# Turning pooled keys and values outside TensorE: block turns, small transfers and the DMA crossbar

## The chip, the cores and the metric

One core of a Trainium2 chip. The metric is the device time of one execution in microseconds (us), median of several runs; lower is better. "The profile" is one profiled execution, "the trace" is what its views are read from. PE is TensorE, PEld its weight loads, DVE VectorE, ACT ScalarE, POOL GpSimd, SP the queue that issues most transfers. A turn is a transposition. The crossbar is the way by which a transfer turns its data (`dma_start_transpose`). The record of an instruction is the duration that the trace gives it, and a transfer has landed when its completion semaphore is full.

## The reference, cut to what matters

```python
B, C, Hh, Ww = (4, 128, 384, 32)          # q: (4, 12288, 128), kv: (4, 384, 32, 128)
kv_pool = kv.reshape(B, H // 4, 4, W // 4, 4, C).mean(axis=(2, 4))
kv_flat = kv_pool.reshape(B, -1, C) @ w_sr               # 768 keys per batch
k = v = kv_flat
a = softmax(q @ k.T / sqrt(C));  x = a @ v               # 49152 tokens of 128
out = (relu(x @ w_gate) * (x @ w_val)) @ w_out           # d_ff = 1536
```

## The kernel before

Tokens go through in 96 tiles of 512, one per loop iteration of 12 steps. A step holds a value and a gate projection, an output product, and scores or attention values. The next batch's keys are prepared on the side, two chunks of 128 keys (a "pair") at a time, three pairs per batch. GpSimd sums the 16 pixels of a key. TensorE turns the sums (`turn_add`), projects them (`project`) and turns the projected keys into values (`turn_values`). Each result goes back from PSUM through VectorE.

```python
def kv_load(b, pair, ...):                  # four transfers of 512 KB, on SP
    ...
        nc.sync.dma_start(parts[:, dh].rearrange("p h dw c -> p (h dw c)"), rows[dh])

def turn_add(b, pair, lines, first, final, chunks=(0, 1)):      # float32, 2 turns for a pair
    ...
            nc.tensor.matmul(kv_Ts[b, pair][:, h], lines[:, h, i], ident, is_transpose=True, ...)
    ...
        nc.vector.tensor_copy(kvT, kv_Ts[b, pair])

def project(b, pair):
    pr = bank([128, 2, 128])
    nc.tensor.matmul(pr, w_sr_f32, kv_Ts.pop((b, pair)), start=True, stop=True)
    nc.vector.tensor_scalar(kv16[:, b, 2 * pair : 2 * pair + 2, 0:C], pr, 1.0 / (r * r), ...)

def turn_values(b, pair):
    vt = bank([128, 2, 128], FP16)
    for h in range(2):
        nc.tensor.transpose(vt[:, h], kv16[:, b, 2 * pair + h, 0:C], ident16)
    nc.vector.tensor_copy(kv16[:, b, 2 * pair : 2 * pair + 2, C : 2 * C], vt)

def x_turn(k):                              # attention output of a tile, by the crossbar, on SP
    ...
    nc.sync.dma_start_transpose(xT, x16.rearrange("p s c -> p (s c)"))

# in the loop (at counts iterations: 0 is where the next batch's keys begin)
if step == 1 and 0 <= at < NJC and at % 2 == 0:
    kv_load(b, at // 2)
if step == 3 and 0 <= at - 2 < NJC:
    pool_pixels(nc.gpsimd, b, (at - 2) // 2, at % 2)
pair = (at - 5) // 2
if at % 2 == 1 and 0 <= pair < NJC // 2:
    if step == 2: turn_open(b, pair); turn_add(b, pair, s3s.pop((b, pair))[:, :, None], True, True)
    if step == 4: project(b, pair)
    if step == 8: turn_values(b, pair)
```

The softmax here doesn't subtract the row's maximum and nothing guards it: scores larger than these inputs give would overflow.

## Time and profile before

| | before |
|---|---|
| time, median of 3 runs | 1048.1 us (1048.07 to 1048.92) |
| span of the profiled run | 1045.5 us, granted TensorE clock 1.000 |
| ordinary iteration | 10.51 us |
| iteration with a pair's turns and projection (nine of them) | 11.28 us |

How to read it: the prediction below shows the lines, and how they say that the time is the length of TensorE's instruction stream.

### The profile page before, as it was taken

Reading aid. Unit: us, or ns where it says so; the run is one execution under the profiler, and the core shown is the slowest. Engines: PE = TensorE matmul, PEld = TensorE weight load, DVE = VectorE, ACT = ScalarE, POOL = GpSimd, SP = SyncE. Lnnn points to the kernel's source line nnn. Section 1 sums busy time; section 2 is a strip of 40 time slices with the busy share of each in tenths; the row PEclk is TensorE's granted clock in tenths of the full one; section 3 lists DMA queues with packets and bytes.
Section 4 is the critical chain, followed back from the end, with each engine's and each line's share of the span. In section 5 each row is a group of like instructions: output and inputs, shape, how many; then the busy total and the mean of one; then the engine's idle time right before and its main releaser. Section 6 shows DMA issues by size and latency. Waiting matters only on the chain.

```text
span 1045.5 us, 25976 instructions
## 1 busy us (share of the span) xinstructions
PE 1036.0 (99%) x9984; PEld 690.1 (66%) x9984; DVE 913.3 (87%) x1679; ACT 908.9 (87%) x1741; POOL 107.8 (10%) x127
## 2 busy tenths in 40 slices
PE   8999999999999999999999999999999999999998
PEld 6566666666666666666666666666666666666665
DVE  3798889898988888998888888889988888888898
ACT  3888888888888888888888888888888888888887
POOL 2000045200000015500000003440000000000000
PEclk9999999999999999999999999999999999999999
DMA  8733256241422335623224134551331322212111
GB/s 302 120 82 74 79 177 167 52 87 32 87 53 65 72 125 138 157 57 72 58 60 87 31 87 132 150 150 41 77 65 53 72 65 54 67 32 67 32 47 47
DMA packets 125853, 90.75 MB, mean 87 GB/s; under 512 B 103328, under 2 KB 104224, under 8 KB 125728
## 3 DMA queue, kind: packets, MB, share of 16 engines
q1 hardware_dynamic: 120144, 75.78, 26.8%
q0 software_dynamic: 5440, 13.24, 7.7%
q8 instruction: 78, 1.28, 0.5%
q14 instruction: 47, 0.39, 0.1%
q10 hardware_dynamic: 144, 0.07, 0.0%
HBM read 52.76 MB, written 25.17 MB: 75 GB/s over the span
## 4 chain that ended last, share of the span: by engine, by line
PE 97%; DMA 1%; SPq 1%; DVE 0%; ACT 0%; issue 0%; DVEq 0%
PE bank_ps L257 25%; PE bank_ps L247 24%; PE bank_ps L236 24%; PE bank_ps L198 12%; PE bank_ps L187 12%; DMA parts<-in_kv_dram 1%; PE bank_ps L156 1%; PE bank_ps L168 1%; SPq L128 0%; ACT aT L188 0%; SPq L93 0%; PE bank_ps L176 0%; DVE kv L169 0%; DVE kvT L163 0%; PE bank_ps L229 0%
## 5 line engine op out<-in xcount | busy, mean ns | idle before, releaser
L250 DVE SCALAR_TENSOR_TENSOR hT<-bank_ps,val 128x512 f16<-128x512 f32 x1152 | 759.5, 687 | 100.9 <-ACT val L240 74.7
L240 ACT CAST val<-bank_ps 128x512 f16<-128x512 f32 x1152 | 677.7, 591 | 111.8 <-PE bank_ps L236 107.5
L257 PEld LDWEIGHTS <-hT 128*128 128x128 f16 x4608 | 351.4, 98 | 200.1 <-issue 0.9
L257 PE MATMUL bank_ps<-wo,hT 128*128 128x128 f16 x4608 | 443.1, 219 | 0.0
L236 PE MATMUL bank_ps<-xT,wv 128*128 128x512 f16 x1152 | 436.6, 379 | 0.0
L247 PE MATMUL bank_ps<-xT,wg 128*128 128x512 f16 x1152 | 435.7, 378 | 0.0
L188 ACT ACTIVATE aT<-bank_ps 128x512 f16<-128x512 f32 x576 | 346.0, 604 | 16.9 <-PE bank_ps L187 16.6
L198 PE MATMUL bank_ps<-kv,aT 128*128 128x129 f16 x2304 | 223.3, 219 | 0.0
L198 PEld LDWEIGHTS <-aT 128*128 128x128 f16 x2304 | 177.2, 98 | 68.1 <-issue 0.6
L187 PE MATMUL bank_ps<-qT,kv 128*128 128x512 f16 x576 | 216.4, 379 | 1.1 <-DVE kv L169 0.5
L247 PEld LDWEIGHTS <-wg 128*128 128x128 f16 x1152 | 111.5, 97 | 65.8 <-issue 0.5
L236 PEld LDWEIGHTS <-wv 128*128 128x128 f16 x1152 | 112.7, 98 | 0.5
L214 DVE TENSOR_TENSOR x<-bank_ps,rinv 128x256 f16<-128x256 f32 x188 | 79.7, 424 | 6.7 <-DVE rinv L206 0.2
L78 POOL DMA_DIRECT2D q<-in_q_dram x23 | 12.5, 545 | 570.6 <-DMA qT<-q 570.4
L275 DVE TENSOR_SCALAR o_sb<-bank_ps 128x512 f32<-128x512 f32 (+1 forms) x95 | 64.0, 674 | 1.3 <-PE bank_ps L257 1.3
L139 POOL TENSOR_TENSOR s<-parts 128x512 f32<-128x512 f32 x36 | 45.3, 1269 | 162.7 <-DMA parts<-in_kv_dram 153.5
L187 PEld LDWEIGHTS <-kv 128*128 128x128 f16 x576 | 55.8, 98 | 2.4 <-DVE kv L169 1.4
L206 DVE RECIPROCAL rinv<-bank_ps 128x2 f32<-128x2 f32 x192 | 30.6, 160 | 1.6 <-PE bank_ps L198 1.6
L141 POOL TENSOR_TENSOR s<-s 128x512 f32<-128x512 f32 x18 | 22.9, 1269 | 1.4
L143 POOL TENSOR_TENSOR c<-s 128x256 f32<-128x256 f32 x18 | 13.1, 726 | 1.4
L163 DVE COPY kvT<-bank_ps 128x256 f32<-128x256 f32 x12 | 5.0, 417 | 4.5 <-PE bank_ps L156 4.5
L146 POOL TENSOR_TENSOR kv_s<-c 128x128 f32<-128x128 f32 x18 | 8.2, 456 | 1.4
(37 smaller groups left out, 81.0 us busy)
## 6 DMA issues: line engine op xcount, KB each, us to landing
parts<-in_kv_dram SPq DMA_DIRECT2D x48, 512.0 KB, 6.4
out_dram<-o_sb SPq DMA_DIRECT2D x95, 256.0 KB, 2.1
q<-in_q_dram POOLq DMA_DIRECT2D x23, 512.0 KB, 5.1
xT<-x SPq DMA_TRANSPOSE x94, 2.5
q<-in_q_dram SPq DMA_DIRECT2D x1, 768.0 KB, 8.3
wv<-in_moe_w_val_dram POOLq DMA_DIRECT2D x2, 192.0 KB, 4.3
wg<-in_moe_w_gate_dram POOLq DMA_DIRECT2D x2, 192.0 KB, 4.9
wo<-in_moe_w_out_dram POOLq DMA_DIRECT2D x1, 384.0 KB, 9.3
```

The costliest lines, as they stand in the source:

```text
L139: eng.tensor_tensor(s2[:, i], parts[:, 2 * i, h], parts[:, 2 * i + 1, h], op=ALU.add)
L187: nc.tensor.matmul(s_ps, kv16[:, k // NST, jc, 0:C], qT_of(k), start=True, stop=True)
L188: nc.scalar.activation(aTs[k][:, jc, :], s_ps, AF.Exp, scale=qk_scale)
L198: nc.tensor.matmul(x_ps[:, i, :], aTs[k][:, jc, s * 128 : (s + 1) * 128], kv16[:, k // NST, jc, C : 2 * C + 1], start=(jc == 0 and i == 0) ...
L206: nc.vector.reciprocal(rinvs[k, half], x_banks[k, half][:, :, C : C + 1])
L214: nc.vector.tensor_tensor(x16s[k][:, 2 * half : 2 * half + 2, :], x_ps[:, :, 0:C], rinv.to_broadcast([128, 2, C]), op=ALU.mult,)
L236: nc.tensor.matmul(va_ps, wv16[:, fb * 128 : (fb + 1) * 128], xTs[k], start=True, stop=True)
L240: nc.scalar.copy(val, va_ps)
L247: nc.tensor.matmul(g_ps, wg16[:, fb * 128 : (fb + 1) * 128], xTs[k], start=True, stop=True)
L250: nc.vector.scalar_tensor_tensor(hTs[k][:, fb, :], g_ps, 0.0, vals.pop((k, fb)), op0=ALU.max, op1=ALU.mult)
L257: nc.tensor.matmul(o_ps, hTs[k][:, fb, s * 128 : (s + 1) * 128], wo16[:, fb, :], start=first, stop=(fb == NFB - 1), skip_group_check=True,)
L275: nc.vector.tensor_scalar(o_sb, o_ps, 1.0 / X_SCALE**2, None, op0=ALU.mult)
```

## The change

Intent: take the turns of the nine later pairs off the bounding engine. VectorE turns the sums in 32x32 blocks, and sixteen transfers of 8 KB put the blocks in place. The values come from the keys by a crossbar transfer per chunk. The key tile is padded so that each chunk has 544 bytes. The projection stays on TensorE and moves to step 10.

```diff
-    kv16 = const.tile([128, B, NJC, 2 * C + 4], FP16)
+    kv16 = const.tile([128, B, NJC, 2 * C + 16], FP16)
...
+    def turn_blocks(b, pair):
+        blocks = work.tile([128, 2, C], FP32, tag="kv_blocks", bufs=2)
+        nc.vector.transpose(
+            blocks.rearrange("p h c -> p (h c)"), s3s.pop((b, pair)).rearrange("p h c -> p (h c)")
+        )
+        kv_Ts[b, pair] = work.tile([128, 2, 128], FP32, tag="kvT", bufs=2, name="kvT")
+        return [(kv_Ts[b, pair], blocks, i, j) for i in range(4) for j in range(4)]
+
+    def block_move(kvT, blocks, i, j):
+        rows, columns = slice(32 * i, 32 * (i + 1)), slice(32 * j, 32 * (j + 1))
+        nc.sync.dma_start(kvT[columns, :, rows], blocks[rows, :, columns])
+
+    def turn_values_dma(b, pair):
+        for jc in (2 * pair, 2 * pair + 1):
+            nc.sync.dma_start_transpose(kv16[:, b, jc, C : 2 * C], kv16[:, b, jc, 0:C])
...
-                pair = (at - 5) // 2
-                if at % 2 == 1 and 0 <= pair < NJC // 2:
-                    if step == 2:
-                        turn_open(b, pair)
-                        turn_add(b, pair, s3s.pop((b, pair))[:, :, None], True, True)
-                    if step == 4:
+                pair, odd = divmod(at - 4, 2)
+                if 0 <= pair < NJC // 2:
+                    if not odd and step == 1:
+                        moves = turn_blocks(b, pair)
+                    if not odd and 2 <= step < 10:
+                        for _ in range(2):
+                            block_move(*moves.pop())
+                    if odd and step == 10:
                         project(b, pair)
-                    if step == 8:
-                        turn_values(b, pair)
+                pair, odd = divmod(at - 6, 2)
+                if 0 <= pair < NJC // 2 and not odd and step == 1:
+                    turn_values_dma(b, pair)
```

More of the change, by code (lines that the diff above doesn't have):

```diff
@@ L310 @@
     nc.gpsimd.tensor_copy(ident16, ident)
-    nc.gpsimd.memset(kv16[:, :, :, 2 * C : 2 * C + 4], 1.0 / X_SCALE)
+    nc.gpsimd.memset(kv16[:, :, :, 2 * C : 2 * C + 16], 1.0 / X_SCALE)
     w_sr_f32 = const.tile([128, C], FP32)
```

## The prediction

> **What bounds the kernel now.** I read the page first (busy shares, the chain that ended last), then the waits, then single stretches of the timeline. The page says TensorE, and says it twice:
>
> ```profile
> PE 1036.0 (99%) x9984; PEld 690.1 (66%) x9984; DVE 913.3 (87%) x1679; ACT 908.9 (87%) x1741; POOL 107.8 (10%) x127
> ...
> PE 97%; DMA 1%; SPq 1%; DVE 0%; ACT 0%; issue 0%; DVEq 0%
> ```
>
> A busy share can mislead, because records of matmuls overlap. So I asked who waited between 100 and 1000 us. In that list TensorE and its weight loads don't occur at all: POOL waits for transfers, ACT waits 98.8 us for TensorE, DVE waits 67.4 us for ACT. TensorE never pauses there, and the time is the length of its instruction stream. The timeline shows that the stream is also dense: each matmul with 512 columns starts 0.215 us after the one before it, and four with 128 columns take 0.22 us. One loop iteration (one token tile) is 12 steps of 0.874 us, or 10.51 us; an iteration that holds the turning and projecting of pooled keys is longer. The windows between stores (188.44, 198.95 and 210.23 us) give both kinds:
>
> ```profile
> 188.44:198.95 10.51, 10.51 (x103) 6.97 (x102) 9.35 (x18) 9.38 (x19) 0.07 (x1) 1.00 0.48 89
> 198.95:210.23 11.28, 11.28 (x109) 7.71 (x108) 10.29 (x21) 9.61 (x19) 0.00 (x0) 1.00 0.13 36
> ```
>
> The columns are the stretch, its length, and busy time of PE, PEld, DVE, ACT and POOL. The second stretch is 0.77 us longer and TensorE fills it. There are nine such stretches (three pairs of key chunks in each of batches 1 to 3). The timeline of TensorE splits the 0.77 us:
>
> ```profile
> 200.75 0.38 PE L156 MATMUL bank_ps<-ident,kv_s 128*128 128x128 f32 x2
> 200.97 0.39 PE L257 MATMUL bank_ps<-wo,hT 128*128 128x128 f16 x4
> ...
> 202.73 0.59 PE L168 MATMUL bank_ps<-kvT,w_sr_f 128*128 128x256 f32 x2
> 203.16 0.39 PE L257 MATMUL bank_ps<-wo,hT 128*128 128x128 f16 x4
> ...
> 206.66 0.27 PE L176 MATMUL bank_ps<-ident,kv 128*128 128x128 f16 x2
> 206.77 0.39 PE L257 MATMUL bank_ps<-wo,hT 128*128 128x128 f16 x4
> ```
>
> The reader is to look at starts, not at lengths: from the start of a group to the start of the next, turning the sums (L156) takes 0.22 us of the stream, the projection (L168) 0.43, turning the values (L176) 0.11; the sum is 0.76 of the 0.77 us.
>
> **What the Trainium skill says.** (1) "TensorE: Matmul & The Clock Gate", section "Part 4: PE-mode transpose": a full 128x128 turn goes to PSUM, so a VectorE copy must follow, and lasts about 275 ns in a kernel. The trace agrees on the record (272 to 273 ns for the float32 turn, 219 ns for the float16 one), but in a full stream a turn delays the next matmul only by 0.11 and 0.055 us. That is what can be won. (2) "VectorE: DVE Perf Modes", section "The three transpose paths": VectorE turns 32x32 blocks only (311 ns for 128x128 of bf16), which is why sixteen block moves must follow; the crossbar does the whole turn. The kernel before has no VectorE turn to compare. (3) "DMA: Bandwidth & Descriptors", section "Anatomy of one DMA": about 2 us of fixed cost in a transfer, mostly completion. The trace agrees: stores land 2.1 us after issue, crossbar turns of 128x512 after 2.5. (4) "Perfetto Trace Analysis", section "Identifying Dependency Chains": an instruction that waits on several engines may get extra semaphore instructions ahead of it. The trace agrees: the projection has one such record of 51 ns on TensorE's queue.
>
> **The change part by part.**
>
> *Removed from TensorE:* in nine places two float32 and two float16 turns: 9 x (0.22 + 0.11) = 2.97 us of a stream without slack. The projection stays (its 9 x 0.43 us as well). The head and batch 0 are untouched.
>
> *VectorE:* per pair it loses two copies (415 and 282 ns) and gains one block turn of 128x256 float32. An instruction with 256 float32 columns here delays the next VectorE instruction by 0.34 us (L214 to the following L250), so I estimate 0.33 to 0.42 us: no more work than before. What matters is the place. The turn stands after the gate product of step 1. VectorE lags TensorE there, since a store's scaling and a normalization came at the end of the iteration before; in the iteration at 210 us it idles again, 0.27 us, before the gate product of step 3. A turn of 0.35 us delays the product of step 2 by that and the one of step 3 by less than 0.1. The matmul that waits for the bank of step 2 starts 0.87 us after that bank is freed, so this is absorbed. The projection's own eviction (415 ns) moves from step 5 to step 10, beside 0.43 us in which TensorE asks VectorE for nothing.
>
> *GpSimd* does the same adds. *The padding* of the key tile costs nothing on the path.
>
> *The SP queue and DMA:* 144 block moves (32 partitions, 2 x 128 bytes each) and 18 crossbar turns. Issuing takes SP 0.34 us for a store and 1.2 us for a turn of four blocks:
>
> ```profile
> 166.65 0.34 SPq L278 DMA_DIRECT2D out_dram<-o_sb  x1
> 167.22 2.15 SPq L222 DMA_TRANSPOSE xT<-x  x1
> 169.47 2.51 SPq L128 DMA_DIRECT2D parts<-in_kv_dram  x4
> 177.16 0.34 SPq L278 DMA_DIRECT2D out_dram<-o_sb  x1
> ```
>
> This is the tightest iteration: the moves of the first pair would follow the loads at 172 us. 16 x 0.34 = 5.4 us of issuing ends at 177.4, about when the next store stands ready. The program has eight completion semaphores for these transfers, so move 9 waits until move 1 has landed; if move 1 queues behind the 2 MB of loads (packets until about 177 us), the moves end near 181 and the next store and turn of tokens go out some 4 us late. A tile's turned tokens are first used some 10 us after its turn is issued (a full iteration lies between), the turn takes 2.5 us to land, and output tiles have three buffers, so this lateness should cost nothing. The projection now comes 18 us after the block turn, so it should find its data.
>
> *TensorE's waits:* this is the part that can take back some gain. In the built program the projection's matmul waits on nine semaphores, eight of them of transfers. They stand in four semaphore instructions (two waits each) ahead of it; before there were two in a pair (one for the first turn, one for the projection). TensorE's single-wait record takes 51 ns; on other engines two waits take up to 2.5 times as long as one (VectorE 21 and 49 ns), so I estimate 0.2 to 0.5 us for the four. Whether that shows depends on how far TensorE's queue runs ahead. I matched each matmul's wait with the time at which its semaphore reached the value. Matmuls that really stall (at 37 to 52 us) start 0.042 us after the release; in the steady part the smallest distance is 0.30 us, and the gate matmul of step 10, just ahead of the projection's new place, has 0.675. From 0.675 I take 0.03 for the wake-up and 0.2 to 0.5: the weights can still be loaded in time. From the smallest distance, 0.30, up to 0.23 us would be lost, nine times 2.1 us. I put 0.3 us in all as the mean of a mostly hidden cost.
>
> **Sum:** 1048.1 - 2.97 + 0.3 = 1045.4 us, a gain of 0.26%.
>
> **The rivals.** *A: the semaphore instructions empty TensorE's queue at each projection.* For it: eight transfer waits ahead of a matmul of the bounding engine. Against: the distance of 0.675 us. It would give 1046 to 1047.5. *B: the SP queue becomes the wait.* For it: 162 more transfers in one queue that also holds the turns of tokens, and the wait of move 9 for move 1. Against: slack of an iteration or more. If moves cost 1 us of issue instead of 0.34, the queue would fall 16 us behind and TensorE would wait for tokens, some us in each of nine places: 1060 to 1080. *C: VectorE falls behind,* because its block turn of float32 is far slower than I assume (1 us, say). Gate products would be 1 us late against 0.8 us of distance; 0.2 us nine times: 1047. *D: the turns were hidden anyway.* Against: each of the nine stretches is longer by just the sum of the three groups. It would give 1048.
>
> **Range and chances.** The most that can be won is 2.97 us, or 0.28%, so faster by 2% is out of reach; slower by 2% needs 21 us, that is B at its worst. Runs of the kernel before spread over 0.85 us. A and C take back up to 2 us. Eight times in 10 I expect 1044.4 to 1047.9. Chances: faster 0.005, within 2% 0.98, slower 0.015.
>
> **What would show it.** Right: the groups of lines 156 and 176 lose 18 matmuls each; the two stretches compared above differ by 0.43 instead of 0.77 us; TensorE still leads the chain with 97%; the waits of the steady part name no TensorE; DVE busy is lower by about 9 x 0.3 us. Wrong: idle time of PE or PEld ahead of the projection, released by a transfer or "issue" (A); ahead of the value matmuls of a later iteration, released by the transfer of turned tokens (B); a block turn of over 0.8 us with matmuls waiting on VectorE behind it (C); moves of much over 0.34 us on the SP queue.

## The result, and the profile after

| | before | after |
|---|---|---|
| median of 6 runs | 1048.43 us (1047.53 to 1050.19) | 1046.24 us (1045.37 to 1048.08) |
| ratio | | 0.998, 95% interval 0.9967 to 0.9993 |
| span of the profiled run | 1045.5 us | 1044.4 us |
| iterations 4 to 92 in the trace | 942.74 us | 941.52 us |
| iterations with a projection | nine of 11.28 us | eight of 10.95 us, one of 12.74 us |

A ratio is the mean time of one kernel's runs over that of the other's runs of the same rounds, so it is not quite the ratio of the medians quoted. "Iterations 4 to 92" runs from the first value-projection matmul of iteration 4 to that of iteration 93 (counted from 0). I use it because the head before the loop differs between profiled runs by 0.8 us (31.9 to 32.7 us), for a reason that no run shows; the profiled spans below contain this difference, and those expected for the experiments do not. Iterations are measured the same way, from first matmul to first matmul.

The profile after, first the busy line and the chain's line of the page (to set beside those in the prediction). Line numbers have moved: 253 is the value projection, 264 the gate, 274 the output product, 168 the projection of keys.

```profile
PE 1032.6 (99%) x9948; PEld 686.1 (66%) x9948; DVE 911.3 (87%) x1670; ACT 907.9 (87%) x1741; POOL 107.9 (10%) x127
...
PE 96%; DMA 2%; SPq 1%; DVE 0%; issue 0%; ACT 0%; DVEq 0%
```

TensorE has lost 36 matmuls and 3.4 us of busy time, but the span is only 1.1 us shorter, and the chain now holds more transfers. In the timeline of TensorE an ordinary pair looks as predicted, with 0.44 us for the projection and nothing else:

```profile
209.04 0.38 PE L264 MATMUL bank_ps<-xT,wg 128*128 128x512 f16 x1
209.25 0.59 PE L168 MATMUL bank_ps<-kvT,w_sr_f 128*128 128x256 f32 x2
209.69 0.39 PE L274 MATMUL bank_ps<-wo,hT 128*128 128x128 f16 x4
```

The first pair of batch 1 does not. The bracket is idle time ahead of the row and what ended it:

```profile
185.78 0.38 PE L264 MATMUL bank_ps<-xT,wg 128*128 128x512 f16 x1
187.37 0.67 PE L168 MATMUL bank_ps<-kvT,w_sr_f 128*128 128x256 f32 x2 [1.21 <-DMA kvT<-blocks]
187.88 0.39 PE L274 MATMUL bank_ps<-wo,hT 128*128 128x128 f16 x4
...
188.76 0.39 PE L274 MATMUL bank_ps<-wo,hT 128*128 128x128 f16 x4
189.32 0.39 PE L253 MATMUL bank_ps<-xT,wv 128*128 128x512 f16 x1 [0.18 <-DMA xT<-x]
```

By starts, the projection comes 1.59 us after the gate matmul where 0.21 is normal, and takes 0.08 longer; at 189.32 another 0.34 us is lost to a late turn of tokens. That is the 1.79 us by which this iteration exceeds the other eight. The two readings close: 9 x 0.33 - 1.79 = 1.18 us, against 1.22 measured over iterations 4 to 92. The medians differ by 2.2 us, more than the traces; the six runs' spans reach from 1043.6 to 1046.2, and the profiled run of before was among its faster ones (1047.35), so I put no weight on the second microsecond.

Why were the moves late? The SP queue's own timeline after, in the stretch whose lines of before are in the prediction:

```profile
167.24 2.39 SPq L239 DMA_TRANSPOSE xT<-x  x1
169.73 2.52 SPq L128 DMA_DIRECT2D parts<-in_kv_dram  x4
172.35 13.72 SPq L190 DMA_DIRECT2D kvT<-blocks  x16
186.17 0.53 SPq L295 DMA_DIRECT2D out_dram<-o_sb  x1
186.81 1.28 SPq L239 DMA_TRANSPOSE xT<-x  x1
```

The store went out at 177.16 us before and goes out at 186.17 now, and the turn of tokens behind it is 9 us late too. The view by line gives what a move costs on SP (duration in ns, minimum, median, maximum) and how long it takes to land:

```profile
L190 SPq DMA_DIRECT2D kvT<-blocks x144: 585/595/1657, 172.3 to 733.0; - x144
...
DMA to landing us min/median/max: 1.7/1.8/7.1
```

A move holds SP 0.595 us, and the next starts 0.64 us after it; sixteen take 10.5 us at the least and 13.72 here, where moves 7 and 8 also wait 2.05 us for completion counters of the pixel loads just ahead: they start 0.02 us after the third and fourth load have landed (178.04 and 179.29 us). Move 9 has a record of 1.66 us. The last move of each pair lands 0.1, 1.8, 2.7 us (batch 1), 1.3, 0.7, 2.8 (batch 2), 0.8, 0.7, 2.3 (batch 3) before the projection's matmul starts. All nine are near the edge; one fell over it in this run.

### The profile page after: what moved, and what is told of

Its sections match the earlier page's. It is cut to its first block, busy times and chain, and to the rows that moved or that the text cites. A ratio compares the mean times of both kernels' runs of the same rounds, so it can differ in the third digit from the quotient of the medians.

```text
span 1044.4 us, 26093 instructions
## 1 busy us (share of the span) xinstructions
PE 1032.6 (99%) x9948; PEld 686.1 (66%) x9948; DVE 911.3 (87%) x1670; ACT 907.9 (87%) x1741; POOL 107.9 (10%) x127
## 4 chain that ended last, share of the span: by engine, by line
PE 96%; DMA 2%; SPq 1%; DVE 0%; issue 0%; ACT 0%; DVEq 0%
PE bank_ps L274 24%; PE bank_ps L264 23%; PE bank_ps L253 23%; PE bank_ps L215 12%; PE bank_ps L204 11%; DMA parts<-in_kv_dram 2%; SPq L128 1%; SPq L190 1%; PE bank_ps L168 0%; PE bank_ps L156 0%; DMA xT<-x 0%; DMA kvT<-blocks 0%; ACT aT L205 0%; SPq L93 0%; DVE kvT L163 0%
## 5 line engine op out<-in xcount | busy, mean ns | idle before, releaser
L168 PE MATMUL bank_ps<-kvT,w_sr_f 128*128 128x256 f32 x24 | 7.5, 393 | 2.1 <-DMA kvT<-blocks 1.2
```

## The experiments

All gave a correct result. The kernel before ran beside them on the same chip (median 1047.94 us of 9 runs; 1047.91 of 10 with the last two).

| kernel | median us (runs) | ratio to before, 95% interval | profiled span | iterations 4 to 92 | iterations with a projection |
|---|---|---|---|---|---|
| before | 1048.43 (6) | | 1045.5 | 942.74 | 9 x 11.28 |
| the change | 1046.24 (6) | 0.998 (0.9967 to 0.9993) | 1044.4 | 941.52 | 8 x 10.95, 12.74 |
| values only | 1046.81 (5) | 0.9989 (0.9976 to 1.0001) | 1044.5 | 941.68 | 9 x 11.16 or 11.17 |
| sums only | 1046.64 (5) | 0.9989 (0.9975 to 1.0003) | 1047.4 | 943.95 | 7 x 10.95, 11.90, 13.20 |
| early loads | 1045.98 (5) | 0.9982 (0.997 to 0.9995) | 1043.2 | 939.72 | 9 x 10.95 |
| half sums | 1042.23 (5) | 0.9945 (0.9933 to 0.9958) | 1040.1 | 936.82 | 9 x 10.62 |
| split moves | 1134.93 (2) | 1.083 (1.081 to 1.085) | 1131.9 | 1028.59 | 18.56 to 23.46 |
| moves by GpSimd | 1046.92 (4) | 0.9989 (0.9973 to 1.0004) | 1044.8 | 941.57 | 7 x 10.95, 11.38, 12.37 |

The theory: the gain is the length of the turns in TensorE's stream, and what is missing of it went into waits that SP's queue makes, since sixteen moves take it 11 us or more. The rivals: the turns were hidden; the crossbar's turns make the queue late; the landing of small transfers is late, not their issue.

### Values only

```diff
-                    if not odd and step == 1:
-                        moves = turn_blocks(b, pair)
...
+                pair = (at - 5) // 2
+                if at % 2 == 1 and 0 <= pair < NJC // 2:
+                    if step == 2:
+                        turn_open(b, pair)
+                        turn_add(b, pair, s3s.pop((b, pair))[:, :, None], True, True)
+                    if step == 4:
                         project(b, pair)
```

> Sums turned by TensorE as before, only the values by the crossbar. Theory (the gain is the length of the turns in TensorE's stream, 0.11 us for two float16 ones): each of the nine iterations with keys lasts 11.17 us instead of 11.28, with no stall, so the span falls by 9 x 0.11 = 1.0 us, to 1044.5. Rival (the turns were hidden, and the gain came from elsewhere, for instance from VectorE's copies): 11.28 us and 1045.5. Rival (the crossbar's turns on the SP queue hold up the turns of tokens): a wait of TensorE for a transfer, span over 1045.5.

Measured: all nine iterations last 11.16 or 11.17 us, no wait of TensorE for a transfer, 942.74 - 941.68 = 1.06 us. The theory holds for this half, and the crossbar's turns alone make nobody late. The reading rests on the trace: as a time, this version cannot be told from before (the interval reaches 1.0001), nor can "sums only" and "moves by GpSimd".

### Sums only

```diff
-                    turn_values_dma(b, pair)
+                    turn_values(b, pair)        # at step 2 of the same iteration
```

> Sums turned by VectorE and sixteen moves, values turned by TensorE. Theory: two float32 turns are 0.22 us of the stream, so an iteration with a projection lasts 10.95 us and the one after it 10.62 (values), 9 x 0.22 = 2.0 us less in all; but the moves still take 11 us or more of the SP queue, so in the first pair of batch 1 the projection waits for the last move as in the changed kernel (1.4 us there, and 0.3 for the late turn of tokens): span about 1045.3. Rival (the crossbar's turns of values, not the moves, make the queue late): no wait for moves, span 1043.5.

Measured: seven iterations of 10.95 us, and after each of the nine one of 10.63 or 10.64: the sums' turns are 0.21 to 0.22 us, as expected. But the first pair of batch 1 waits again (11.90), and that of batch 3 loses 2.25 us (13.20). With two waits the kernel lost more in this profiled run than it gained; the run is the slowest of its five, and of the other four no trace was kept. The crossbar's turns of values are not what is needed for lateness. TensorE's timeline around the second wait:

```profile
695.48 0.38 PE L264 MATMUL bank_ps<-xT,wg 128*128 128x512 f16 x1
696.33 0.67 PE L168 MATMUL bank_ps<-kvT,w_sr_f 128*128 128x256 f32 x2 [0.47 <-DVE hT L267]
...
697.71 0.39 PE L274 MATMUL bank_ps<-wo,hT 128*128 128x128 f16 x4
699.48 0.39 PE L253 MATMUL bank_ps<-xT,wv 128*128 128x512 f16 x1 [1.38 <-DMA xT<-x]
```

The second row teaches something about reading. The bracket names VectorE, but the first of the four semaphore instructions ahead of this matmul, which waits on two transfers' counters, took 1.11 us there instead of 0.051, and the last move landed 0.41 us before the matmul. The matmul waits for several semaphores, and the view names the wrong one.

### Early loads

```diff
-                if step == 1 and 0 <= at < NJC and at % 2 == 0:
-                    kv_load(b, at // 2)
+                if step == 1 and 0 <= at + 1 < NJC and at % 2 == 1:
+                    kv_load(b, (at + 1) // 2)
```

> The whole change, with each pair's pixels loaded one iteration earlier, so that no loads stand ahead of the moves of the first pair in the SP queue. Theory (the queue is late by the sum of 16 x 0.64 us of issuing and 2.7 us in which moves 7 and 8 wait for completion counters of the loads, so the loads tip the balance): the moves start near 169.5 us and end near 181, margin of the first projection over 3 us, the waits of 1.2 and 0.2 us are gone, all nine iterations last 10.95 us, span 1042.6. Rival (issuing alone is enough to be late): a wait of 1 us or more for moves remains in at least one pair, span over 1043.5.

Measured: nine iterations of 10.95 us, TensorE absent from the list of waits between 100 and 1000 us, and 942.74 - 939.72 = 3.02 us over iterations 4 to 92: the whole predicted 2.97. SP's timeline in the same stretch:

```profile
167.42 0.34 SPq L295 DMA_DIRECT2D out_dram<-o_sb  x1
167.99 1.31 SPq L239 DMA_TRANSPOSE xT<-x  x1
170.10 10.36 SPq L190 DMA_DIRECT2D kvT<-blocks  x16
180.57 0.53 SPq L295 DMA_DIRECT2D out_dram<-o_sb  x1
```

The moves end at 180.47 instead of 186.07 us. (The 2.7 us of the expectation run from the end of move 6 to the start of move 8; by starts the wait is the 2.05 us named above.) The least margin of any projection over its last move is 1.2 us, the least of any value projection over its turned tokens 0.7. I expected over 3 us for the first projection and found 3.5; the other margins stay at 1.2 to 4.1, so the queue is still close to its limit. As a time, 1045.98 us cannot be told from the 1046.24 of the change: the trace shows the stall gone, the clock on the wall doesn't resolve 1.8 us.

### Half sums

```diff
-            s3s[b, pair] = work.tile([128, 2, C], FP32, tag="kv_s3", ...)
+            s3s[b, pair] = work.tile([128, 2, C], FP16, tag="kv_s3", ...)
+    def turn_sums_dma(b, pair):                  # in place of turn_blocks and block_move
+        kv_Ts[b, pair] = work.tile([128, 2, 128], FP16, tag="kvT16", bufs=2, name="kvT16")
+        nc.sync.dma_start_transpose(kv_Ts[b, pair], s3.rearrange("p h c -> p (h c)"))
+    def project16(b, pair):
+        nc.tensor.matmul(pr, w_sr16, kv_Ts.pop((b, pair)), start=True, stop=True)   # float16
...
+    nc.gpsimd.tensor_copy(w_sr16, w_sr_f32)      # once, in the head
```

> The sums kept in float16, turned by one crossbar transfer per pair, and projected in float16 (no block turn, no moves). Theory: the projection of 256 columns takes 0.11 us of the stream in float16 instead of 0.43, and the turns are gone, so the nine iterations last 10.62 us instead of 11.28 and the span falls by 9 x 0.66 = 5.9 us, to 1039.6; no wait for transfers, since the SP queue carries three turns per pair instead of sixteen moves and two turns. Rival (the float16 projection is no shorter in the stream): 10.95 us, 1042.5. The result must stay within tolerance, as the projected keys are float16 in any case.

Measured: nine iterations of 10.62 us, 942.74 - 936.82 = 5.92 us, no wait. The timeline shows the projection by starts at 0.11 us:

```profile
186.31 0.38 PE L263 MATMUL bank_ps<-xT,wg 128*128 128x512 f16 x1
186.53 0.27 PE L186 MATMUL bank_ps<-kvT,w_sr 128*128 128x256 f16 x1
186.64 0.39 PE L273 MATMUL bank_ps<-wo,hT 128*128 128x128 f16 x4
```

This version is the fastest of all here: 0.9945 of before, its interval clear of that of the change, and its five runs lie within 0.64 us. It trades nothing that the check could see, but its sums and the projection's weights are rounded to float16 before the projection.

### Split moves

```diff
-        nc.sync.dma_start(kvT[columns, :, rows], blocks[rows, :, columns])
+        for h in range(2):
+            nc.sync.dma_start(kvT[columns, h, rows], blocks[rows, h, columns])
```

> The whole change, with each block move split in two (one per chunk of keys): 32 moves of 4 KB per pair instead of 16 of 8 KB, the same bytes and the same result. Theory (a move costs the SP queue about 0.64 us whatever its size): 32 moves take 20.5 us, some 29 us of SP work in two iterations of 21.5, so the first projection of a batch waits about 10.5 us for moves and each of the next two about 7.5; 25 us per batch, 75 in all, near 1120 us. Rival (issuing goes with bytes or rows moved): 32 x 0.32 us, the moves end when they did, and the time stays at 1046.

Measured: 1134.93 us, 8.3% slower. SP's view by line and timeline:

```profile
L191 SPq DMA_DIRECT2D kvT<-blocks x288: 507/589/1722, 172.4 to 821.2; - x144
...
172.41 23.89 SPq L191 DMA_DIRECT2D kvT<-blocks  x32
```

Half the bytes cost the same 0.589 us, and 32 moves take 20.6 us at the least. The loads of 512 KB on the same queue have a median of 0.589 us too (in the kernel before). So issuing has a price per transfer, not per byte. The first projection waits 10.9 us (10.5 expected). The nine pauses, of 5.4 to 10.9 us, add up to 67.4 us, less than the 75 expected, yet iterations 4 to 92 are 86 us longer than before. The windows of this run show the other cost (the columns are again the stretch, its length and busy times of PE, PEld, DVE, ACT and POOL; the number ahead of DMA share and GB/s is the granted clock):

```profile
186.00:197.50 11.50, 0.81 (x6) 0.20 (x3) 1.38 (x2) 1.31 (x3) 2.44 (x3) 0.67 0.05 8
197.50:203.80 6.30, 6.23 (x33) 4.08 (x34) 3.00 (x6) 2.26 (x4) 0.47 (x1) 0.53 0.87 205
203.80:210.00 6.20, 6.20 (x63) 4.08 (x60) 5.46 (x10) 5.21 (x11) 0.10 (x1) 1.00 0.62 102
```

After the pause TensorE runs for about 6 us at half its clock: matmuls of 512 columns start 0.43 us apart instead of 0.215. By the trace's record of the clock, it stays at half for 3.4 to 5.9 us behind each of the nine pauses, 41 us in all. Half of that is lost, an estimate of 20.6 us, and 67.4 + 20.6 - 2.97 = 85.0 of the 85.9 us are accounted for. The Trainium skill has this in "TensorE: Matmul & The Clock Gate", section "Why this matters for your kernels": a TensorE gap of more than about 3 us brings the clock down to half. This trace agrees for pauses of 10.9 us and 5.4 us (granted clock 0.53 and 0.62 in the stretch behind), and the 1.4 us pause of the change did not do it (the window from 187.73 to 198.70 us has 1.00). No run here has a pause between 1.6 and 5.4 us in the loop, so where the limit lies is not tested.

### Moves by GpSimd

```diff
-        nc.sync.dma_start(kvT[columns, :, rows], blocks[rows, :, columns])
+        nc.gpsimd.dma_start(kvT[columns, :, rows], blocks[rows, :, columns])
```

> The whole change, with the sixteen moves issued by GpSimd instead of SP. Theory (the stall is made by SP's queue, not by the transfers themselves): SP issues the turn of tokens as early as in the kernel before, the waits of TensorE for turned tokens are gone, and if a move costs GpSimd no more than the 0.55 us that its loads of queries cost, 16 of them and its 10 us of adds fit in two iterations of 21.5 us: all nine iterations 10.95 us, span 1042.6. Rival (landing of small transfers behind the loads is what is late): the first projection of batch 1 still waits 1 us or more. Third possibility: a move costs GpSimd 0.8 us or more, then GpSimd is the late one and the projections wait for it in every pair.

Measured: the waits for turned tokens are gone (least margin 1.6 us), and seven iterations last 10.95 us, but the first projection of batch 1 waits 0.4 us and that of batch 3 1.4. A move costs GpSimd 0.539 us, so the price was not the trouble. GpSimd's timeline at the first pair of batch 1:

```profile
170.16 1.13 POOL L190 DMA_DIRECT2D kvT<-blocks  x2 [24.89 <-DVE blocks L182]
171.31 2.51 POOL L139 TENSOR_TENSOR s<-parts 128x512 f32<-128x512 f32 x2
...
176.04 0.46 POOL L146 TENSOR_TENSOR kv_s<-c 128x128 f32<-128x128 f32 x1
176.44 6.39 POOL L190 DMA_DIRECT2D kvT<-blocks  x12
183.55 1.07 POOL L190 DMA_DIRECT2D kvT<-blocks  x2 [0.71 <-DMA kvT<-blocks]
```

Two moves go out, then 5 us of adds for the next pair, then fourteen. The in-order queue of another engine has other work in it, and the last move is again late. But this order alone doesn't make it late. The second pair of each batch has the same adds between its moves and no pixel loads ahead of them, and its last move lands 1.2 to 1.5 us before the projection:

```profile
192.15 1.11 POOL L190 DMA_DIRECT2D kvT<-blocks  x2 [1.49 <-PE bank_ps L264]
193.27 2.50 POOL L139 TENSOR_TENSOR s<-parts 128x512 f32<-128x512 f32 x2
...
198.40 7.45 POOL L190 DMA_DIRECT2D kvT<-blocks  x14
```

In the first pair of batch 1 the moves also land late: the last two are held up 0.71 us until earlier ones have landed, and the very last lands 2.61 us after its issue instead of 1.6. In that of batch 3, 2.3 us pass between moves 10 and 11, and the profile does not show why. So late landing, the rival, has a part in the waits that remain; this run does not separate it from the order. In the pairs without adds in between (the third of each batch) the moves take 8.5 us and land 6 us early.

## Why the prediction was right, point by point

**The removed turns: right.** 9 x (0.22 + 0.11) us was the term, and the iterations show 0.33 us each in eight of nine. The two halves come out alone (0.11 in "values only", 0.21 to 0.22 in "sums only"), so the turns were not hidden (rival D falls).

**VectorE: right.** The block turn has a record of 433 ns (estimated 330 to 420), and no matmul of the steady part waits for VectorE behind it: eight of nine pairs lose nothing, so rival C falls. (The list of waits names VectorE once, 1.7 us at the weight load of the late projection; that is the wait for the moves, seen above.) I expected VectorE's busy time to fall by 2.7 us; it fell by 2.0.

```profile
L182 DVE STREAM_TRANSPOSE blocks<-kv_s x9: 433/433/434, 168.9 to 720.8; 128x256 f32<-128x256 f32 x9
```

**TensorE's waits: right that they hide, and now sized.** The four semaphore instructions start 0.105 to 0.111 us apart in the trace where nothing is late, 0.44 us in all, inside the estimated 0.2 to 0.5. In the pair of the timeline above the first starts at 208.40 us, 0.85 us ahead of the matmul that it guards, and nothing is lost. They cost time only where the last move is late: in "split moves" the projection starts 0.135 us after the last landing where the last counter stands in the fourth instruction, 0.24 us in the third, 0.46 us in the first. Rival A as a cost of its own falls.

**The SP queue: this is the term that was mis-sized.** The step read "16 x 0.34 = 5.4 us of issuing ends at 177.4", and from it "the moves end near 181" and "it should find its data". A move takes 0.595 us of record and 0.64 from start to start, so sixteen take 10.5 to 13.7, and in the tightest iteration they ended at 186.07. I had taken the 0.34 of a store that has the queue to itself. All 97 stores of the kernel before are issued 0.7 us or more after the transfer ahead has left the queue, and their records are 0.33 to 0.36 us. After the change eleven stores follow another transfer within 0.12 us, and theirs are 0.53 us or more, as at 186.17 us above. So 0.34 was not the price in a run of transfers, not even for a store. The line beside it in my own fence had the better one: four loads into SBUF in 2.51 us, 0.63 each. Two errors of slack follow. The projection does come 18 us after the block turn, but only 0.1 to 2.8 us after its last data have landed. And the turned tokens, whose lateness "should cost nothing", landed at the worst 0.05 us before their first matmul, which had waited 0.34 us for them. So rival B happened in small, once in this trace, and cost 1.79 us.

**The sum: the number came out with a mis-sized term in it, and with some luck.** I put 0.3 us for waits, and 1.8 were lost in the profiled run, for another reason than the one that I put it down to. The trace gained 1.2 us over iterations 4 to 92 where the sum says 2.7; the medians gained 2.2. That the queue, at almost twice the issue time that I had put down, cost no more is luck: the other eight projections had 0.7 to 2.8 us to spare, and "split moves" shows what lies beyond. The range of 3.5 us was wide enough for this. The signs that I named in advance for B (idle time of value matmuls, released by turned tokens; moves far over 0.34 us) are those that appeared, and "the waits of the steady part name no TensorE" was wrong.

**Small slips.** Twelve steps of 0.874 us make 10.49; a step is 0.876. Point (1) on the skill sets the page's 275 ns, which is for bf16, beside a float32 turn. The float16 turn, of two bytes as well, has a record of 219 ns, so page and trace agree less well than the text says.

What stays open: why a transfer that follows another holds SP 0.53 us (a store) or 0.59 (into SBUF) and a store after a pause only 0.34. Splitting shows only that the size of the transfer is not it. It is open too why in eight of the nine pairs one move or more has a record of 0.8 to 1.7 us. How often the stall occurs in runs without a stored trace isn't known either.

## What to carry to other kernels

Where one engine's stream is dense, a removed instruction is worth its distance from start to start, not its record, and such sums came out within 0.1 us here (3.02 for 2.97, 1.06 for 1.0, 5.92 for 5.9). Work that is moved to transfers is paid per transfer in an in-order queue: take the issue time of a transfer of the same kind (here into SBUF) from the profile, where it follows another transfer without a pause, multiply, and compare with the time until the next thing in that queue is due, landing included. If the data can be two bytes wide, one crossbar transfer replaces sixteen block moves, and the product that follows is shorter too.

## What the Trainium skill lacked or had wrong

- "DMA: Bandwidth & Descriptors", section "Issuing engines are not separate DMA queues", says that the sequencer's time to start a transfer is usually small relative to the transfer. For moves of 8 KB it is a third: 0.64 us of SP against 1.8 us to land, and since transfers overlap and issuing doesn't, the issue is what limits: sixteen took 10.4 us or more, and 4 KB cost the same 0.59 us. The page has no issue time by kind (0.34 us for a store after a pause and 0.53 right behind another transfer, 0.59 into SBUF, 1.22 for a crossbar turn of one 128x128 block and 1.20 of four).
- "TensorE: Matmul & The Clock Gate", section "Part 4: PE-mode transpose", gives a turn's duration only, for bf16. In a full stream a turn cost 0.055 us (float16) and 0.11 us (float32).
- "VectorE: DVE Perf Modes", section "The three transpose paths", has no float32 case: 433 ns for 128x256.
- "Perfetto Trace Analysis", section "Identifying Dependency Chains", mentions the extra semaphore instructions without a price: here 0.11 us each on TensorE's queue with two waits, free while the queue runs ahead.
